# Softmax denominators of 83 of 128 attention units: from four one-column matmuls to a DMA transpose and a VectorE sum

## The chip, the cores and the metric

The kernel runs on one core of a Trainium2 chip. The metric is the device time of one execution in microseconds (us); the median of three runs of the kernel before is 1280.31 us (1280.17 to 1280.67). A profiled execution gives the durations that are used below.

The engines are named as in the profile: PE is TensorE (matmuls), PEld its weight loads, DVE is VectorE, ACT is ScalarE, POOL is GpSimd, and SP is the engine that issues most of the DMAs (SPq is its queue, which works strictly in the order of the program). Each engine works through its own instructions in program order and waits at an instruction until what it needs is there.

## The reference, cut to what matters

```python
xn = layernorm(x)                                   # x: 2048 x 512
q  = (xn @ wq) -> 32 heads x 2048 x 128
p  = softmax(q @ k_cache^T * 128**-0.5)             # 32 heads, 2048 keys
s  = (p @ v_cache) -> 2048 x 4096, then @ wo        # attention
g  = silu(B(xn))                                    # a token-shift mixer and an MLP, gelu
out = x + s * g
```

The change concerns the softmax only. The kernel computes exp(score) without a maximum, multiplies it with V unnormalised, and divides the result afterwards by the sum of the exponentials over the 2048 keys. That sum, the denominator, is one number per query.

## The kernel before, in words

**Units and slots.** The attention is cut into 128 *units* of one head and 512 queries, in the order `units = (g, qt, hh)`: eight groups g of four heads, in each four query blocks qt, in each four heads hh. A unit has eight *slots* (SPU), and a slot treats two key chunks of 128 keys. The main loop (line 695) runs over all 1024 slots n = 8u + p. I write 33.4 for slot 4 of unit 33. What is called from the loop is pinned in program order, so the loop body writes the order of every engine's queue by hand; `at(n, fn)` hangs further work on the end of slot n.

In each slot PE does two score matmuls (`s_slot`, into one of two PSUM tiles of the pool psS; ACT then writes exp of both, 128x1024, into pT) and two matmuls with V (`pv_slot`) of the slot LAG = 5 places earlier, into a PSUM tile `ps_o` (psO, two of them). A pT tile holds two slots; there are four. Further matmuls stand in given slots:

- slots 0 and 1: the query projection of unit u+2 (`q_mm`, four matmuls). `q_copy` brings it to SBUF at slot 2, on DVE, and on ACT for the last units (u+2 > QUIET+1 = 122).
- slot 3: `sums` of unit u-1, four matmuls (below).
- slots 4 and 5: the output projection of an earlier query block (`wo_mm`, four matmuls), evicted by `wo_post` on DVE at slot 6. Such work is put into `wo_todo` after `norm` of a block's fourth head.
- slots 2, 3 and slots 6, 7 are two windows; in each there may be one chunk of the other branch (mixer and MLP), four or five matmuls. There are 136 chunks and some 230 windows. A pair of chunks of the stage m3 (ps_m<-xn2T) ends in a gelu made by hand: `pre` and `square` on ACT, `poly` on DVE two slots later, `tanh` on ACT two slots after that, `last` on DVE after two more. ACT's `tanh` waits for `poly`, and the exponentials stand behind it.

**The denominators.** DVE adds the eight pT quarters of a unit up: `add_first` at slot 4, `add_next` at slot 6, `add_last` (three additions, lines 205, 210, 211) at slot 0 of the next unit. What remains, acc, is 128 keys x 512 queries. `sums` (line 223) multiplies each quarter of acc (128 columns in steps of 4) with a column of ones: four matmuls with one column each, the result 128 x 4 in PSUM. `recip` (line 231) takes the reciprocal on DVE and sends it to DRAM (dr<-rc); `bcast` (line 248, slot 4) reads it back to all 128 partitions (rb<-dr, 128x512); `norm` (line 253) at slot 2 of the unit after multiplies ps_o with rb on DVE and thus frees that PSUM tile for the unit after next.

**PSUM tags.** Two single tiles are left, "xa" and "xm". q_mm, sums and wo_mm share xa; the chunks use xm. From unit 120 on, `sums` uses xm.

**Loads.** K comes by transposing DMAs in four pieces, V in two halves, all issued by SP; a `todo` hung on a slot gives their place in SP's queue. At the start the normalised tokens are turned by SP's transposing DMA too (`ln1_turn`, xnT<-xn); unit 2's slots 6 and 7 hold the first `q_mm` that needs tokens 512 to 1023.

Of the kernel before, what the change touches and what calls it, by code (L numbers as in the profile page):

```python
# [9 lines left out]
ALU = mybir.AluOpType  # L10
FP32 = mybir.dt.float32
# [6 lines left out]
def kernel(  # L18
# [15 lines left out]
    nc = tc.nc  # L34
# [17 lines left out]
    NG = H // HG  # L52

    SPU = KC // 2
    LAG = 5
    KSPLIT = 4
    KJ = KC // KSPLIT
    BASE_J = [3, 3, 2, 2]
# [30 lines left out]
    wqp = ent(pool("wqp", HG + 2))  # L89
    wop = ent(pool("wop", 2 * HG))  # L90
    qtp = ent(pool("qt", 4))
    ptp = ent(pool("pt", 4))
    trp = ent(pool("tr", 2))
    rp = ent(pool("rp", 2))
    otp = ent(pool("ot", 2))
    smp = ent(pool("smp", 4))
    gtp = ent(pool("gt", 2))
# [26 lines left out]
    LQ = QT - 1  # L124
    deferred = {(NG - 2, qt): qt for qt in (LQ - 1, LQ)}
    NS = NU * SPU
    kTs, vBs, wqs, wos, oTs, st = {}, {}, {}, {}, {}, {}
    todo = defaultdict(list)

    def at(n, fn):  # L130
        todo[n].append(fn)
# [35 lines left out]
    def q_mm(u, dcs):  # L167
        g, qt, hh = units[u]
        if dcs[0] == 0:
            st[u] = dict(psq=psX.tile([P, 512], FP32, tag="xm" if u == HG else "xa", name="ps_q"))  # L170
        for dc in dcs:
            mm(st[u]["psq"][:], wqs[g * HG + hh][:, dc, :],
               xnT[:, dc, qt * 512:(qt + 1) * 512], dc == 0, dc == DC - 1)
# [49 lines left out]
    def sums(u):  # L223
# [4 lines left out]
            mm(ps[:, j:j + 1], a[:, j, :], ones_t[:], True, True)  # L228
        recip(s, ps)

    def recip(s, ps):
        rc = smp.tile([P, 4], FP32, name="rc")
        pin(nc.vector.reciprocal(out=rc[:], in_=ps[:]))  # L233
        s["dr"] = drp.tile([P, 4], FP32, name="dr")
        pin(nc.sync.dma_start(out=s["dr"][:], in_=rc[:]))
# [17 lines left out]
    def norm(u, pieces=1):  # L253
        g, qt, hh = units[u]
        s = st.pop(u)
        if hh == 0:
            oTs[(g, qt)] = otp.tile([P, HG, 512], BF16, name="oT")
        w = 512 // pieces
        for i in range(pieces):
            c = slice(i * w, (i + 1) * w)  # L260
            pin(nc.vector.tensor_tensor(  # L261
                out=oTs[(g, qt)][:, hh, c], in0=s["o"][:, c], in1=s["rb"][:, c], op=ALU.mult))
# [94 lines left out]

    def ln1_norm(t):
        xin = ln.pop(t)
        xn = tokp.tile([P, D], BF16, tag="tb", bufs=8, name="xn")  # L360
        norm1(t, xn[:], xin[:])
        return xn

# [121 lines left out]
            lambda: hT[:, 2 * jp:2 * jp + 2, b + tt * 512: b + (tt + 1) * 512])  # L485

    def xn_load(t):
        mlp["xnext"] = tokp.tile([P, D], BF16, tag="tb", bufs=8, name="xr")
        nc.gpsimd.dma_start(out=mlp["xnext"][:], in_=xsrc[t])

    def m2_chunk(t):
# [90 lines left out]
    def m4_chunk(t, part):  # L582
        fcs = list(M4[part])
        ts = t % 4

        def run(i, n):
            if part == 0 and i == 0:
                mlp["ps"] = psX.tile([P, 512], FP32, tag="xm", name="ps_m")
                mlp["xr"] = tokp.tile([P, D], BF16, tag="tb", bufs=8, name="xr")
                nc.gpsimd.dma_start(out=mlp["xr"][:], in_=x1_d[t][:])  # L590
            h = (len(fcs) + 1) // 2
            for fc in (fcs[:h], fcs[h:])[i]:
                mm(mlp["ps"][:], mlp["h2"][fc // 2][:, fc % 2, ts * P:(ts + 1) * P],
                   mlp["w4"][fc][:], fc == 0, fc == FC - 1)
            if part == 2 and i == 1:
                ps, xr = mlp["ps"], mlp["xr"]
                th = tokp.tile([P, D], BF16, tag="th", bufs=1, name="th")

                def x2():
                    pin(nc.vector.scalar_tensor_tensor(  # L600
                        out=xr[:], in0=ps[:], scalar=0.5, in1=xr[:], op0=ALU.mult, op1=ALU.add))

                def tanh():
                    pin(nc.scalar.activation(out=th[:], in_=xr[:], func=ACT.Tanh, scale=0.5))

                def silu():
                    pin(nc.vector.scalar_tensor_tensor(  # L607
                        out=xr[:], in0=th[:], scalar=1.0, in1=xr[:], op0=ALU.add, op1=ALU.mult))
                    nc.gpsimd.dma_start(out=g_d[t][:], in_=xr[:])  # L609

                at(evict(n), x2)
                at(n + 3, tanh)
                at(soft(n + 5), silu)
        return run
# [49 lines left out]
    for t, (stats, apply, turn) in enumerate(tokens, 4):  # L664
# [2 lines left out]
        at(stats, lambda t=t: ln1_stats(t))  # L667
        at(apply, lambda t=t: ln1_apply(t))
        at(turn, lambda t=t: ln1_turn(t))
    for n, h, piece in ((2, 2, 2), (4, 2, 3), (12, 3, 0), (15, 3, 1), (17, 3, 2), (20, 3, 3)):  # L670
        at(n, lambda h=h, piece=piece: load_k(h, (piece,)))
    for n, h, half in ((7, 2, 0), (13, 2, 1), (20, 3, 0), (21, 3, 1)):
        at(n, lambda h=h, half=half: load_v(h, (half,)))
    at(28, ph1_load)
    at(64, w2_load)
# [2 lines left out]
    for g in range(NG - 1):  # L678
        b = (g * QT + QT - 1) * HG
        for hh in range(HG):  # L680
            h = (g + 1) * HG + hh
            for i in range(KSPLIT):
                at((b - 2 + (2 * hh + i // 2 + (hh > 0))) * SPU + (5, 7)[i % 2], lambda h=h, i=i: load_k(h, (i,)))
            for i in range(2):
                at((b - 2 + (2 * hh + i + (hh > 0))) * SPU + 6, lambda h=h, i=i: load_v(h, (i,)))
            at((b + (-4, -4, -1, -1)[hh]) * SPU + (5, 7)[hh % 2], lambda h=h: load_w(h))
            at((b - 4 - hh // 2) * SPU + (5, 7)[hh % 2], lambda h=h: load_wo(h))

# [3 lines left out]
            at((QUIET + 1 + 2 * (t % 4)) * SPU + 4, lambda t=t: gate_sum(t))  # L692

    wo_todo = deque()
    for n in range(NS):
        u, p = divmod(n, SPU)
        s_slot(u, p)
        m = n - LAG
        if m >= 0:
            pv_slot(*divmod(m, SPU))  # L700
        if u == 0 and p in (1, 3, 5):
            q_mm(1 + p // 2, range(DC))
        if u == 0 and p in (2, 4, 6):
# [8 lines left out]
            add_last(u - 1)  # L712
        if p == 2 and HG - 1 <= u < NU - 2:
            q_copy(u + 2)
        if p == 2 and u >= 2:
            norm(u - 2)
            gg, qq, hh = units[u - 2]
            if hh == HG - 1 and (gg, qq) in deferred:
                pin(nc.sync.dma_start(out=o_d[qq][:], in_=oTs[(gg, qq)][:]))
            elif hh == HG - 1:  # L720
                wo_todo.extend((gg, 4 * qq + ts) for ts in range(4))
                if gg == NG - 1:
                    fin_load(4 * qq)
        if p == 3 and u >= 1:
            sums(u - 1)
        if p == 4 and u >= 1:
            bcast(u - 1)
        if p in (4, 5) and wo_todo:
            wo_mm(*wo_todo[0], (0, 1) if p == 4 else (2, 3))
        if p == 6 and QUIET <= u < NU - 1:  # L730
            add_next(u, 2)
        if p == 6 and wo_todo:
            gg, t = wo_todo.popleft()
            wo_post(gg, t)
            if gg == NG - 1:
                at(n + 5, lambda t=t: wo_out(t))
                if t % 4 < 3:
                    fin_load(t + 1)
        if p == 4:
            add_first(u)  # L740
        if p == 4 and u == NU - 1:
            a = st[u]["acc"]
            pin(nc.vector.tensor_tensor(out=a[:, 0:2, :], in0=a[:, 0:2, :], in1=a[:, 2:4, :], op=ALU.add))
        if p == 6 and u < QUIET:
            add_next(u, 2)
        if p in (2, 3, 6, 7):
# [54 lines left out]
        wo_part(dst[j], GL, ts[j], range(HG), False, True)  # L801
    for j in range(4):
        last_scale(ts[j], dst[j])
        if j < 2:
            last_out(ts[j], nc.gpsimd)
    for j in (2, 3):
        last_out(ts[j], nc.vector)
    ph.close()

# [29 lines left out]
```

## Time and profile before

| what | value |
|---|---|
| median of 3 runs | 1280.31 us |
| the profiled execution's own time | 1279.53 us |
| its span in the trace | 1277.8 us |
| granted TensorE clock, mean | 0.999 |
| PSUM sum matmuls (ps_sum<-ones_t,acc) | 516 of them, 171 ns each, 34.3 us busy |
| multiply by the reciprocal (oT<-ps_o,rb, 128x512) | 127 of them, 680 ns each |
| transposing DMAs SBUF to SBUF (xnT<-xn, xn2T<-x1r) | 12 and 16, 3.8 us to landing in the median |
| transposing DMAs of K | 128, 4.7 us to landing in the median |

Matmuls are pipelined: one of 512 columns lasts 0.38 us in the records, but the next begins 0.216 us later. A PE that is called busy is therefore read by its starts: a stretch in which every 512-column matmul starts 0.216 us after the one before has no wait in it. A row of the timeline joins instructions of one kind that follow each other (x2, x4) and shows the time from the first start to the last end.

### The profile page before, as it was taken

What the parts mean: (1) busy time and instruction counts of PE and PEld (TensorE: products, weight loads), DVE (VectorE), ACT (ScalarE), POOL (GpSimd) and SP (SyncE); (2) the same over time, 40 slices, a digit from 0 to 9 for tenths busy, and PEclk for the clock granted to TensorE, in tenths of its full rate; (3) what the DMA queues carried; (4) which work ended last, traced back from release to release, by engine and by line L of the source; (5) the groups of instructions that cost most, each with busy time, mean ns of one, the idle gap of its engine ahead of it and who ended that gap; (6) DMA issues with size and microseconds to landing.
All of it is one profiled execution on the core that took longest, in us unless ns stands there. A gap on an engine that the chain in (4) does not pass through costs nothing.

```text
span 1277.8 us, 17233 instructions
## 1 busy us (share of the span) xinstructions
PE 1257.1 (98%) x6195; PEld 612.1 (48%) x6320; DVE 1019.2 (80%) x1407; ACT 1113.0 (87%) x1195; POOL 137.9 (11%) x241
## 2 busy tenths in 40 slices
PE   8999999999999999999999999999999999999998
PEld 5444444444444444444444444444444444444444
DVE  7888889898788877778887778887777888777886
ACT  7899998888999988899988889998888999888883
POOL 4430003323110010000001000000000000000110
PEclk9999999999999999999999999999999999999999
DMA  9644343455532564134443244523435133542532
GB/s 185 133 106 81 59 79 88 108 124 123 115 77 67 100 110 89 42 75 83 89 93 68 58 85 93 96 42 75 96 80 90 34 70 72 91 105 46 140 76 58
DMA packets 172950, 111.79 MB, mean 87 GB/s; under 512 B 124800, under 2 KB 149888, under 8 KB 172864
## 3 DMA queue, kind: packets, MB, share of 16 engines
q1 hardware_dynamic: 163904, 85.51, 34.3%
q0 software_dynamic: 8672, 24.91, 7.9%
q8 instruction: 49, 0.80, 0.3%
q14 instruction: 37, 0.30, 0.1%
q10 hardware_dynamic: 288, 0.26, 0.1%
HBM read 82.58 MB, written 7.60 MB: 71 GB/s over the span
## 4 chain that ended last, share of the span: by engine, by line
PE 87%; ACT 6%; DVE 4%; issue 1%; DMA 1%; POOL 0%; DVEq 0%; ACTq 0%
PE ps_s L114 31%; PE ps_o L114 30%; PE ps_m L114 9%; PE ps_wo L114 8%; PE ps_q L114 7%; ACT pT L194 4%; PE ps_sum L114 1%; ACT sq L425 1%; DVE acc L205 1%; ACT pre L455 1%; DVE bn L349 0%; DMA rb<-dr 0%; DMA xnT<-xn 0%; DVE acc L210 0%; DVE qT L180 0%
## 5 line engine op out<-in xcount | busy, mean ns | idle before, releaser
L194 ACT ACTIVATE pT<-ps_s 128x1024 bf16<-128x1024 f32 x1024 | 1012.0, 1031 | 141.0 <-PE ps_s L114 130.0
L114 PE MATMUL ps_s<-qT,kT 128*128 128x512 bf16 x2004 | 599.5, 379 | 4.1 <-ACT pT L194 1.0
L114 PE MATMUL ps_o<-pT,vb 128*128 128x512 bf16 x1997 | 597.6, 379 | 2.8
L205 DVE TENSOR_TENSOR acc<-acc,pT 128x2048 bf16<-128x2048 bf16 x254 | 309.8, 1220 | 65.5 <-ACT pT L194 60.8
L114 PEld LDWEIGHTS <-kT 128*128 128x128 bf16 x2048 | 226.8, 113 | 224.4 <-issue 18.6
L114 PEld LDWEIGHTS <-vb 128*128 128x128 bf16 x2048 | 199.8, 98 | 225.2
L200 DVE TENSOR_TENSOR acc<-pT 128x2048 bf16<-128x2048 bf16 x128 | 155.9, 1218 | 26.6 <-ACT pT L194 26.4
L114 PE MATMUL ps_q<-xnT,wq_h 128*128 128x512 bf16 (+1 forms) x519 | 150.7, 374 | 3.3 <-DMA xnT<-xn 2.0
L114 PE MATMUL ps_wo<-wo_h,oT 128*128 128x512 bf16 x456 | 136.3, 379 | 0.6
L328 DVE TENSOR_TENSOR s_acc<-ps_wo,s_acc 128x512 f32<-128x512 f32 x100 | 68.9, 689 | 73.9 <-PE ps_wo L114 71.0
L210 DVE TENSOR_TENSOR acc<-acc 128x1024 bf16<-128x1024 bf16 x127 | 87.9, 692 | 4.4
L261 DVE TENSOR_TENSOR oT<-ps_o,rb 128x512 bf16<-128x512 f32 x129 | 87.1, 676 | 4.1 <-DMA rb<-dr 4.0
L180 DVE CAST qT<-ps_q 128x512 bf16<-128x512 f32 x122 | 83.5, 685 | 4.8 <-PE ps_q L114 4.8
L114 PEld LDWEIGHTS <-wq_h 128*128 128x128 bf16 x524 | 50.6, 98 | 63.2 <-issue 3.6
L114 PEld LDWEIGHTS <-oT 128*128 128x128 bf16 x480 | 46.9, 98 | 57.7 <-issue 2.6
L114 PE MATMUL ps_m<-xn2T,w_sb 128*128 128x512 bf16 x222 | 66.1, 378 | 0.2
L114 PE MATMUL ps_m<-w_sb,h2T 128*128 128x512 bf16 x218 | 62.7, 379 | 0.2
L577 POOL DMA_DIRECT2D w_sb<-in_B_w_dram x28 | 21.1, 756 | 353.8 <-PE ps_m L114 328.6
L211 DVE TENSOR_TENSOR acc<-acc 128x512 bf16<-128x512 bf16 x127 | 54.0, 425 | 4.3
L233 DVE RECIPROCAL rc<-ps_sum 128x4 f32<-128x4 f32 x128 | 22.9, 179 | 40.9 <-PE ps_sum L114 40.0
L114 PEld LDWEIGHTS <-acc 128*128 128x128 bf16 x516 | 37.6, 115 | 29.6 <-issue 1.5
L609 POOL DMA_DIRECT2D g_d<-xr x16 | 8.8, 547 | 346.3 <-DVE xr L607 346.3
(74 smaller groups left out, 599.9 us busy)
## 6 DMA issues: line engine op xcount, KB each, us to landing
rb<-dr SPq DMA_DIRECT2D x128, 256.0 KB, 4.1
vb<-in_A_v_cache_dram SPq DMA_DIRECT2D x64, 256.0 KB, 4.5
w_sb<-in_B_w_dram POOLq DMA_DIRECT2D x28, 256.0 KB, 4.6
wo_h<-in_A_wo_dram SPq DMA_DIRECT2D x32, 128.0 KB, 3.9
wq_h<-in_A_wq_dram SPq DMA_DIRECT2D x28, 128.0 KB, 4.2
kT<-in_A_k_cache_dram SPq DMA_TRANSPOSE x128, 4.7
dr<-rc SPq DMA_DIRECT2D x128, 2.0 KB, 1.4
xr<-in_A_x_dram POOLq DMA_DIRECT2D x16, 128.0 KB, 3.5
```

What stands on the lines that cost most here:

```text
L114: pin(nc.tensor.matmul(out=out, lhsT=lhsT, rhs=rhs, start=start, stop=stop))
L180: pin(nc.vector.tensor_copy(out=qT[:], in_=st[u].pop("psq")[:]))
L194: pin(nc.scalar.activation(out=s["pT"][-1][:, jj:jj + 2, :], in_=sps[:], func=ACT.Exp, scale=SCALE))
L200: pin(nc.vector.tensor_tensor(out=s["acc"][:], in0=s["pT"][0][:], in1=s["pT"][1][:], op=ALU.add))
L205: pin(nc.vector.tensor_tensor(out=a[:], in0=a[:], in1=st[u]["pT"][i][:], op=ALU.add))
L210: pin(nc.vector.tensor_tensor(out=a[:, 0:2, :], in0=a[:, 0:2, :], in1=a[:, 2:4, :], op=ALU.add))
L211: pin(nc.vector.tensor_tensor(out=a[:, 0, :], in0=a[:, 0, :], in1=a[:, 1, :], op=ALU.add))
L233: pin(nc.vector.reciprocal(out=rc[:], in_=ps[:]))
L261: pin(nc.vector.tensor_tensor(out=oTs[(g, qt)][:, hh, c], in0=s["o"][:, c], in1=s["rb"][:, c], op=ALU.mult))
L328: pin(nc.vector.tensor_tensor(out=sa, in0=ps[:], in1=sa, op=ALU.add))
L425: pin(nc.scalar.activation(out=sq[:], in_=pre[:], func=ACT.Square, scale=GELU_A ** 0.5))
L577: pin(nc.gpsimd.dma_start(out=w[:], in_=w3_v[:, :, fc * P:(fc + 2) * P]))
```

## The change

Units T0 = 32 to T1 - 1 = 114, 83 of them, are "turned". For these, `sums` is not called. Instead the folded acc (128 keys x 512 queries, bf16) is transposed by a DMA that SP issues at slot 2 of the next unit (`acc_turn`); at slot 6 DVE adds each of the 4 x 128 rows up along the keys (`turned_sums`), then `recip` as before. `bcast` moves from slot 4 of the next unit to slot 1 of the unit after, `norm` from slot 2 to slot 6 of that unit. Query q = 128 j + p now lies at place 4 p + j of rb, so that `norm` reads rb in steps of four.

Because `norm` comes later, V matmuls run up to eight slots behind: the lag grows 5, 6, 7, 8 in slots 33.1, 33.3 and 33.5, and shrinks again in 117.3, 117.7 and 118.3. pT has five tiles instead of four; rb one instead of two; the token tiles "tb" four instead of eight. V halves of three of a group's four heads are hung three slots later. `wo_post` asks whether a projection is in PSUM (wo_box) rather than whether one is to be done. The last query projections (u > 122) use tag xm instead of xa. Three of the first loads move to later slots, and of the last four output additions one instead of two is on POOL.

```diff
-    LAG = 5
-    ptp = ent(pool("pt", 4))
+    ptp = ent(pool("pt", 5))
-    rp = ent(pool("rp", 2))
+    rp = ent(pool("rp", 1))
+    atp = ent(pool("at", 1))
+    T0, T1 = 8 * HG, NU - 13
+    LAGS = [((T0 + 1) * SPU + 1, 5), ((T0 + 1) * SPU + 3, 6), ((T0 + 1) * SPU + 5, 7),
+            ((T1 + 2) * SPU + 3, 8), ((T1 + 2) * SPU + 7, 7), ((T1 + 3) * SPU + 3, 6), (NS, 5)]
...
-            st[u] = dict(psq=psX.tile([P, 512], FP32, tag="xm" if u == HG else "xa", name="ps_q"))
+            st[u] = dict(psq=psX.tile([P, 512], FP32, tag="xm" if u == HG or u > QUIET + 1 else "xa", name="ps_q"))
...
+    def turned(u):
+        return T0 <= u < T1
+
+    def acc_turn(u):
+        s = st[u]
+        s["at"] = atp.tile([P, 4, P], BF16, name="accT")
+        pin(nc.sync.dma_start_transpose(out=s["at"][:], in_=s["acc"][:, 0, :]))
+
+    def turned_sums(u):
+        s = st[u]
+        sm = smp.tile([P, 4], FP32, name="sm")
+        pin(nc.vector.tensor_reduce(
+            out=sm[:], in_=s.pop("at")[:], axis=mybir.AxisListType.X, op=ALU.add))
+        recip(s, sm)
...
+        if turned(u):
+            f = "x (j p) -> x j p"
+            pin(nc.vector.tensor_tensor(
+                out=oTs[(g, qt)][:, hh, :].rearrange(f, j=4), in0=s["o"].rearrange(f, j=4),
+                in1=s["rb"].rearrange("x (p j) -> x j p", j=4), op=ALU.mult))
+            return
...
-    for n, h, piece in ((2, 2, 2), (4, 2, 3), (12, 3, 0), (15, 3, 1), (17, 3, 2), (20, 3, 3)):
+    for n, h, piece in ((2, 2, 2), (4, 2, 3), (14, 3, 0), (16, 3, 1), (17, 3, 2), (20, 3, 3)):
-    for n, h, half in ((7, 2, 0), (13, 2, 1), (20, 3, 0), (21, 3, 1)):
+    for n, h, half in ((7, 2, 0), (15, 2, 1), (20, 3, 0), (21, 3, 1)):
...
-                at((b - 2 + (2 * hh + i + (hh > 0))) * SPU + 6, lambda h=h, i=i: load_v(h, (i,)))
+                at((b - 2 + (2 * hh + i + (hh > 0))) * SPU + (9 if hh else 6), lambda h=h, i=i: load_v(h, (i,)))
...
-        m = n - LAG
-        if m >= 0:
-            pv_slot(*divmod(m, SPU))
+        lag = next(v for lim, v in LAGS if n < lim)
+        while pv_done <= n - lag:
+            pv_slot(*divmod(pv_done, SPU))
+            pv_done += 1
...
-        if p == 2 and u >= 2:
+        if u >= 1 and p == 2 and turned(u - 1):
+            acc_turn(u - 1)
+        if u >= 2 and p == 1 and turned(u - 2):
+            bcast(u - 2)
+        if u >= 2 and p == (6 if turned(u - 2) else 2):
             norm(u - 2)
...
-        if p == 3 and u >= 1:
+        if p == 3 and u >= 1 and not turned(u - 1):
             sums(u - 1)
-        if p == 4 and u >= 1:
+        if p == 4 and u >= 1 and not turned(u - 1):
             bcast(u - 1)
...
-        if p == 6 and wo_todo:
+        if p == 6 and wo_box:
             gg, t = wo_todo.popleft()
             wo_post(gg, t)
...
+        if p == 6 and u >= 1 and turned(u - 1):
+            turned_sums(u - 1)
         if p == 6 and u < QUIET:
             add_next(u, 2)
...
     for j in range(4):
         last_scale(ts[j], dst[j])
-        if j < 2:
+        if j == 0:
             last_out(ts[j], nc.gpsimd)
-    for j in (2, 3):
+    for j in range(1, 4):
         last_out(ts[j], nc.vector)
```

More of the change, by code (lines that the diff above doesn't have):

```diff
@@ L359, in ln1_norm @@
         xin = ln.pop(t)
-        xn = tokp.tile([P, D], BF16, tag="tb", bufs=8, name="xn")
+        xn = tokp.tile([P, D], BF16, tag="tb", bufs=4, name="xn")
         norm1(t, xn[:], xin[:])
@@ L487, in xn_load @@
     def xn_load(t):
-        mlp["xnext"] = tokp.tile([P, D], BF16, tag="tb", bufs=8, name="xr")
+        mlp["xnext"] = tokp.tile([P, D], BF16, tag="tb", bufs=4, name="xr")
         nc.gpsimd.dma_start(out=mlp["xnext"][:], in_=xsrc[t])
@@ L588, in run @@
                 mlp["ps"] = psX.tile([P, 512], FP32, tag="xm", name="ps_m")
-                mlp["xr"] = tokp.tile([P, D], BF16, tag="tb", bufs=8, name="xr")
+                mlp["xr"] = tokp.tile([P, D], BF16, tag="tb", bufs=4, name="xr")
                 nc.gpsimd.dma_start(out=mlp["xr"][:], in_=x1_d[t][:])
@@ L694 @@
     wo_todo = deque()
+    pv_done = 0
     for n in range(NS):
```

## The prediction

> **What bounds the kernel now.** I read the page's busy shares and its chain of work, then the timeline unit by unit.
>
> ```profile
> PE 1257.1 (98%) x6195; PEld 612.1 (48%) x6320; DVE 1019.2 (80%) x1407; ACT 1113.0 (87%) x1195; POOL 137.9 (11%) x241
> ...
> PE 87%; ACT 6%; DVE 4%; issue 1%; DMA 1%; POOL 0%; DVEq 0%; ACTq 0%
> ```
>
> The chain runs through PE. Counting PE's weight loads unit by unit gives the test: number of 512-column matmuls times 0.216 us, plus the four sum matmuls, against the unit's length. Most units agree within 0.02 us (unit 23: 44 x 0.216 + 0.13 = 9.63 of 9.63); others exceed it by 0.1 to 0.3. So a matmul taken away shortens the run, except where PE already waits. What a denominator costs is seen in unit 34, slots 2 to 4:
>
> ```profile
> 342.63 1.94 ACT L194 ACTIVATE pT<-ps_s 128x1024 bf16<-128x1024 f32 x2 [0.33 <-PE ps_s L114]
> 342.80 0.59 PE L114 MATMUL ps_s<-qT,kT 128*128 128x512 bf16 x2
> ...
> 343.23 0.59 PE L114 MATMUL ps_o<-pT,vb 128*128 128x512 bf16 x2
> 343.45 0.40 PEld L114 LDWEIGHTS <-acc 128*128 128x128 bf16 x4
> 343.66 0.27 PE L114 MATMUL ps_sum<-ones_t,acc 128*128 128x1 bf16 x4
> 343.76 0.15 PEld L114 LDWEIGHTS <-kT 128*128 128x128 bf16 x2
> 343.79 0.60 PE L114 MATMUL ps_s<-qT,kT 128*128 128x512 bf16 x2
> ```
>
> The scores follow the first sum by 343.79 - 343.66 = 0.13 us: four one-column matmuls at 0.033 each, not the 171 ns of the table. That, not 34 us, is at stake.
>
> **A. The sums removed.** 83 x 0.13 = 10.9 at most. But a score pair may not start before the exponential two slots earlier has ended, plus 0.05 us (the least distance in the trace). Above, that exponential ends at 342.63 + 1.03 = 343.66, so without the sums the scores start at 343.71 instead of 343.66: a gain of 0.08. In 49 of the slots after a removed sum the distance is 0.75 or more (a chunk filled slots 2, 3): 49 x 0.131 = 6.4; in 34 it is short and 0.07 to 0.09 is left: 2.7. Together **-9.1**.
>
> **B. The lag.** In 33.1, 33.3 and 33.5 no V pair is issued; 3 x 0.432 = 1.30 us of PE work is done later, in 117.3 to 118.3. Unit 33 cannot use the free time: ACT runs without a pause from 33.1 to 33.6 (ACT is busy 9.80 of the unit's 9.84 us). Following its exponentials, PE leaves unit 33 only 0.27 earlier, of which 0.07 stands in A. **+1.1** (0 to 1.3).
>
> **C. The first loads.**
>
> ```profile
> 29.54 1.19 SPq L370 DMA_TRANSPOSE xnT<-xn  x1
> ...
> 33.98 0.59 PE L114 MATMUL ps_q<-xnT,wq_h 128*128 128x512 bf16 x2 [1.96 <-DMA xnT<-xn]
> ...
> 35.55 1.12 SPq L146 DMA_TRANSPOSE kT<-in_A_k_cache_dram  x1
> 36.73 1.08 SPq L156 DMA_DIRECT2D vb<-in_A_v_cache_dram  x2
> ```
>
> PE waits 2 us for the last token block. Taking a K piece (1.25 of SP) and a V half (0.6 and the gap) out of SP's way brings its turn 2.0 earlier, from 29.54 to 27.5. What is late next: V of head 3 is issued at 36.73 and lands 4.5 later, 41.2, behind the same sum of SP work as now; PE's first V matmul of unit 3 stands at 41.80. So only some 0.5 survives; **-0.4** (0 to -2.0).
>
> **D. Output projections** come one unit later for turned blocks. Mostly a swap; unit 109, which waits 0.59 for ACT with only four matmuls in slots 4 and 5, gets four more there. **-0.5** (0 to -0.6).
>
> **E. The end of attention.** q in tag xm no longer waits for the eviction of xa (0.46 of excess in each of 123.0 and 125.0): -0.9. But the sums of these units are in xm too, and stand after q:
>
> ```profile
> 1200.40 0.59 PE L114 MATMUL ps_o<-pT,vb 128*128 128x512 bf16 x2
> 1200.71 0.59 ACT L178 ACTIVATE qT<-ps_q 128x512 bf16<-128x512 f32 x1
> 1200.83 0.27 PE L114 MATMUL ps_sum<-ones_t,acc 128*128 128x1 bf16 x4
> ...
> 1215.40 0.59 PE L114 MATMUL ps_q<-xnT,wq_h 128*128 128x512 bf16 x2 [0.51 <-DVE s_acc L328]
> ```
>
> The sums must now await q's copy: 1200.71 + 0.59 + 0.05 - 1200.83 = 0.5 in units 121 to 125, everything on PE behind them: +2.6. Net **+1.7**. The last additions: POOL's cost 1.15, DVE's 0.68 without POOL beside it (692 ns for an fp32 addition); three in a row on DVE end about 0.15 later: **+0.15** (-0.4 to +0.4).
>
> **F. What DVE and SP get.** Per turned unit DVE loses nothing (the reciprocal stays) and gets a sum over 128x512 bf16. The trace has no such operation; rows with 512 elements take 425 (bf16 addition) to 689 ns (eviction), a statistics pass over 512 bf16 679. I take 0.68, being a reduction too; upper end 1.22, the row of twice the elements. The multiply reads rb in steps of 16 bytes: no VectorE row has steps. The nearest is a PE weight load, 113 ns in steps (kT) against 98 (vb), so 0.68 x 1.15 = 0.78; ends 0.68 and, twice as long, 1.36. It moves into the 0.75 to 1.3 us in which DVE idles before the eviction of slot 6, so it costs little even then. DVE's average load rises from 40.4 to about 44 of 49 us in the five heaviest units, 33 to 37. But order matters:
>
> ```profile
> 366.91 0.69 DVE L328 TENSOR_TENSOR s_acc<-ps_wo,s_acc 128x512 f32<-128x512 f32 x1 [1.30 <-PE ps_wo L114]
> ...
> 367.72 1.22 DVE L205 TENSOR_TENSOR acc<-acc,pT 128x2048 bf16<-128x2048 bf16 x1
> ...
> 368.86 1.22 DVE L429 SCALAR_TENSOR_TENSOR sq<-sq,pre 128x1024 bf16<-128x1024 bf16 x1
> ...
> 370.27 1.10 ACT L434 ACTIVATE sq<-sq 128x1024 bf16<-128x1024 bf16 x1
> ```
>
> Sum and reciprocal (0.71 + 0.10) come between the first two rows, which have 0.2 of slack: poly ends 0.6 later, at 370.68. Tanh, now 0.2 behind poly, starts 0.47 later, the exponentials behind it too, and PE waits 0.28 for the second (372.29 + 0.47 + 0.05 against 372.53). Eight m3 pairs close in slots 2, 3 with this slack of 0.20; the other four have 0.5 to 0.8 and the 16 in slots 6, 7 at least 1.0 with norm gone from before poly. 8 x 0.28 = **+2.2** (0 to +4).
>
> SP's queue gets 83 transposes of 1.2 us issue each; a unit has 9.6 and no unit fills it. Their path: add_last ends (362.56 in unit 36), landing 3.8 later in the median of the SBUF transposes (2.4 to 6.2), DVE wants the data at 367.5, 4.9 after. rb is issued some 2 us after the reciprocal, lands 4.1 later and is wanted 7 after. Each psO tile is free more than a slot before V needs it at lag 8. So all of it is hidden: 0, with the next paragraph's rival behind it. DMA shares are 0.42 and rise by 83 x 0.66 / 1278 = 4 points (512 packets of about 20 ns on 16 engines).
>
> **Sum**: -9.1 + 1.1 - 0.4 - 0.5 + 1.7 + 0.15 + 2.2 = -4.85. The profiled execution took 1279.53 (span 1277.8), so 1274.7; the median of runs lies 0.8 above it, so **1275.4**.
>
> **Rivals.** *Late transposes (slower).* The turn waits for DVE, lands, and DVE waits for it with everything behind it: add_next, poly, so ACT's tanh and the exponentials. Up to 4.9 us of landing is free (4.3 after a gelu). From then on each us hits the 12 pairs of slots 2, 3; at 5.4 the gain is gone (12 x 0.4), at 5.8 as a median 0.9 is late: 12 x 0.8 = 9.6, 1285; beyond 6 the 16 other pairs join. For: K's median is 4.7, its longest 7.0. Against: SBUF sources 3.8. Chance 0.16.
>
> *DVE dearer than rows of 512 elements.* With 1.22 for the sum, poly is 0.54 later still: 8 x 0.54 + 4 x 0.4 = 5.9, so 1281; with 1.36 for the multiply alone, 1 at most, in units like 33. Chance 0.15 between 1277.5 and 1282. [...]
>
> *ACT as the bound.* If in the 47 turned units with m3 chunks (ACT 94% busy) nothing were gained, A shrinks by about 5: 1280.3. Against: PE's starts follow at 0.216 in most of their slots. Chance 0.08.
>
> *Better.* If poly's delay hides and the start gains 2.0: 1275.4 - 2.2 - 1.6 = 1271.6. Chance 0.14 below 1273.
>
> Forecast itself, 1273 to 1277.5: 0.47. A run of this kernel can tell 0.2%, 2.6 us. Faster by more (below 1277.75): 0.47 + 0.14 + 0.02; slower (above 1282.9): the late transposes, 0.15; the rest, 0.22, within. The range takes in the better case and the dear sum: 1271 to 1282.5.
>
> **What would show it.** Right: no ps_sum between 33.3 and 115.3; units without a gelu 0.13 or 0.08 shorter; a wait of ps_sum in 121 to 125; tanh of eight pairs starting 0.5 later; accT landing near 3.8. Wrong: DVE's sum waiting for accT, a multiply over 1 us, score pairs waiting for ACT in most units.

## The result, and the profile after

The changed kernel takes 1285.91 us in the median (1283.88 to 1287.36, six runs), the kernel before 1280.49 (1279.83 to 1281.34) beside it: a ratio of 1.0042 (1.0032 to 1.0052). It is slower by 5.4 us, where 4.9 less was forecast. The profiled execution took 1285.89, its span is 1284.1 and its mean granted clock 0.997.

The page's busy shares and chain of work, in answer to the two lines of before:

```profile
PE 1253.0 (98%) x5870; PEld 602.0 (47%) x5988; DVE 1096.0 (85%) x1491; ACT 1113.4 (87%) x1195; POOL 137.7 (11%) x240
...
PE 70%; ACT 10%; DVE 8%; DMA 7%; issue 3%; SPq 1%; POOL 0%; DVEq 0%; ACTq 0%
```

PE's sums are gone from the matmul count, but the share of PE in the chain fell from 87% to 70%; ACT, DVE and DMA took it. DVE has 77 us more to do. So PE does less and waits more. Where, the length of stretches of units tells (from the weight loads of the unit's first score matmuls, as in the prediction). The same table serves the experiments:

| kernel (profiled execution) | 0-5 | 6-32 | 33-115 | 116 | 117-118 | 121-125 |
|---|---|---|---|---|---|---|
| before | 52.67 | 266.36 | 819.75 | 8.99 | 19.46 | 45.67 |
| **after** | 57.28 | 266.38 | 816.10 | 11.60 | 20.76 | 47.02 |
| after_again | 53.47 | 266.41 | 822.64 | 10.63 | 20.76 | 47.03 |
| after_third | 53.49 | 266.36 | 819.67 | 10.78 | 20.76 | 47.03 |
| before_nosums | 52.95 | 266.40 | 810.74 | 8.99 | 19.46 | 45.67 |
| before_lags | 53.02 | 266.40 | 820.31 | 9.02 | 20.75 | 45.64 |
| after_freered | 53.38 | 266.40 | 815.45 | 9.06 | 20.76 | 47.03 |
| after_bare | 52.76 | 266.36 | 811.92 | 9.02 | 20.76 | 45.65 |
| after_late_units | 53.06 | 266.34 | 815.96 | 9.02 | 19.50 | 45.65 |

After against before: +4.61 at the start, -3.65 in the units with removed sums, +2.61 in unit 116, +1.30 where the lag shrinks, +1.35 at the end; together +6.2 of the 6.36 between the two profiled executions. Three places of it need their lines.

**The turned units.** The sums are gone as meant. Unit 34 again, slots 1 to 3, from the timeline: the scores follow each other at once.

```profile
346.50 0.38 PE L114 MATMUL ps_s<-qT,kT 128*128 128x512 bf16 x1
...
347.36 0.59 PE L114 MATMUL ps_s<-qT,kT 128*128 128x512 bf16 x2
```

The distance from 346.50 to 347.36 is four matmuls of 0.216 (two of scores, two with V) and nothing else. But two units on, DVE is late. The timeline of units 34 to 37, DVE, SP, ACT and PE in order of time (start, duration, instruction, idle time before it and what ended it); the write of unit 33's reciprocals (dr) and its broadcast (rb) come first:

```profile
353.11 0.32 SPq L253 DMA_DIRECT2D dr<-rc  x1
353.47 1.13 SPq L149 DMA_TRANSPOSE kT<-in_A_k_cache_dram  x1
357.31 0.32 SPq L268 DMA_DIRECT2D rb<-dr  x1
...
361.96 1.08 DVE L278 TENSOR_TENSOR oT<-ps_o,rb 128x512 bf16<-128x512 f32 x1 [1.76 <-DMA rb<-dr]
...
368.78 0.42 DVE L214 TENSOR_TENSOR acc<-acc 128x512 bf16<-128x512 bf16 x1
369.24 1.21 SPq L240 DMA_TRANSPOSE accT<-acc  x1
...
373.75 0.69 DVE L245 TENSOR_REDUCE sm<-accT 128x4 f32<-128x512 bf16 x1 [1.23 <-DMA accT<-acc]
...
375.68 1.22 DVE L453 SCALAR_TENSOR_TENSOR sq<-sq,pre 128x1024 bf16<-128x1024 bf16 x1
...
377.00 1.06 ACT L458 ACTIVATE sq<-sq 128x1024 bf16<-128x1024 bf16 x1 [1.92 <-DVE sq L453]
377.96 2.84 ACT L197 ACTIVATE pT<-ps_s 128x1024 bf16<-128x1024 f32 x3
...
379.02 0.59 PE L114 MATMUL ps_s<-qT,kT 128*128 128x512 bf16 x2 [1.66 <-ACT pT L197]
```

The same places in the kernel before, unit 33's write and broadcast and the end of unit 35's additions:

```profile
344.18 0.32 SPq L235 DMA_DIRECT2D dr<-rc  x1
345.58 0.32 SPq L250 DMA_DIRECT2D rb<-dr  x1
345.95 1.12 SPq L146 DMA_TRANSPOSE kT<-in_A_k_cache_dram  x1
...
362.14 0.42 DVE L211 TENSOR_TENSOR acc<-acc 128x512 bf16<-128x512 bf16 x1
```

This is a cascade. It begins at rb: in the changed kernel a K piece now stands between write and broadcast, the write of units 32 and 33 lands after 3.95 and 4.14 us (1.40 and 1.39 before), and rb, which waits for it, is issued 4.2 after the write instead of 1.4. In the two other profiles of the changed kernel below these landings are 3.1 to 4.5. That the K piece slows the write is not shown; and late writes alone do not stop PE, since after_bare (below) has them too, 4.23 and 3.80, and exceeds its matmuls by only 0.26 and 0.43 in units 36 and 37. The multiply of unit 33 then waits 1.76 for rb; everything that DVE has behind it is late, the additions of unit 35 too. They end 6.3 us into unit 36, where in the kernel before they ended 4.0 into it. So the transpose is issued late (369.24), lands 4.5 later (the median of all 83 is 3.6), and the sum waits 1.23 for it. Poly stands behind the sum, ACT's tanh waits 1.92 for poly, the exponentials stand behind tanh, and PE waits 1.66.

**Unit 116.** A late accT meets the change back to matmul sums:

```profile
1146.20 1.23 SPq L240 DMA_TRANSPOSE accT<-acc  x1
...
1152.21 0.69 DVE L245 TENSOR_REDUCE sm<-accT 128x4 f32<-128x512 bf16 x1 [1.98 <-DMA accT<-acc]
...
1156.65 0.68 DVE L183 CAST qT<-ps_q 128x512 bf16<-128x512 f32 x1
1157.39 0.27 PE L114 MATMUL ps_sum<-ones_t,acc 128*128 128x1 bf16 x4 [2.42 <-DVE qT L183]
```

The last transpose lands 6.0 after its issue, the sum waits 1.98, the copy of q comes late, and the first matmul sums after the turned units share tag xa with that q: 2.42 of waiting.

**The start.** The timelines of SP and of PE:

```profile
36.87 0.32 SPq L268 DMA_DIRECT2D rb<-dr  x1
...
38.42 1.08 SPq L159 DMA_DIRECT2D vb<-in_A_v_cache_dram  x2
```

```profile
39.94 0.59 PE L114 MATMUL ps_s<-qT,kT 128*128 128x512 bf16 x2
44.04 1.03 PE L114 MATMUL ps_o<-pT,vb 128*128 128x512 bf16 x2 [3.51 <-DMA vb<-in_A_v_cache_dram]
44.87 1.06 PE L114 MATMUL ps_s<-qT,kT 128*128 128x512 bf16 x2
```

V of head 3 was issued at 38.42 (36.73 before) and landed 5.6 later instead of 4.5; PE, which no longer waits 2 us for the tokens, was there at 40.5 and idled for 3.51. After that two matmuls take 0.83 from start to start instead of 0.43. The busy time of the engines in stretches of 2 us says why (after the five engines: granted clock, share of the DMA engines, GB/s):

```profile
44.00:46.00 2.00, 1.96 (x5) 0.73 (x6) 1.97 (x5) 0.03 (x1) 0.41 (x1) 0.50 0.36 64
46.00:48.00 2.00, 2.00 (x6) 0.75 (x5) 0.60 (x1) 1.32 (x2) 1.85 (x3) 0.50 0.35 49
```

The granted clock fell to 0.50 at 43.3, while PE still idled, and stayed there for 6.83 us. PE was at work in 6 of them, at half its rate, which costs another 3.0 (an estimate: half of 6).

The measured prices of the new operations, from the page's groups (count, then busy time and mean ns, then idle time before them):

```profile
L278 DVE TENSOR_TENSOR oT<-ps_o,rb 128x512 bf16<-128x512 f32 x83 | 89.2, 1075 | 17.5 <-DMA rb<-dr 17.5
L245 DVE TENSOR_REDUCE sm<-accT 128x4 f32<-128x512 bf16 x83 | 56.3, 678 | 4.1 <-DMA accT<-acc 3.9
```

The sum takes 678 ns, the multiply with rb in steps of 16 bytes 1075 instead of 680; and DVE waits 17.5 us for rb (23 times), where the multiplies of the kernel before waited 3.6 in all.

### The profile page after: what moved, and what is told of

The parts are those of the page before. It is cut to its first block, busy times and chain, and to the rows that moved or that the text cites. A ratio compares the mean times of both kernels' runs of the same rounds, so it can differ in the third digit from the quotient of the medians.

```text
span 1284.1 us, 16634 instructions
## 1 busy us (share of the span) xinstructions
PE 1253.0 (98%) x5870; PEld 602.0 (47%) x5988; DVE 1096.0 (85%) x1491; ACT 1113.4 (87%) x1195; POOL 137.7 (11%) x240
## 4 chain that ended last, share of the span: by engine, by line
PE 70%; ACT 10%; DVE 8%; DMA 7%; issue 3%; SPq 1%; POOL 0%; DVEq 0%; ACTq 0%
PE ps_s L114 26%; PE ps_o L114 25%; ACT pT L197 8%; PE ps_m L114 7%; PE ps_wo L114 7%; PE ps_q L114 6%; DVE acc L208 3%; DMA accT<-acc 2%; DMA dr<-rc 2%; DMA rb<-dr 2%; ACT pre L479 1%; DVE sm L245 1%; ACT sq L458 1%; DVE acc L213 1%; DVE oT L278 1%
## 5 line engine op out<-in xcount | busy, mean ns | idle before, releaser
L114 PEld LDWEIGHTS <-kT 128*128 128x128 bf16 x2048 | 229.8, 113 | 240.0 <-issue 29.9
L278 DVE TENSOR_TENSOR oT<-ps_o,rb 128x512 bf16<-128x512 f32 x83 | 89.2, 1075 | 17.5 <-DMA rb<-dr 17.5
L245 DVE TENSOR_REDUCE sm<-accT 128x4 f32<-128x512 bf16 x83 | 56.3, 678 | 4.1 <-DMA accT<-acc 3.9
L453 DVE SCALAR_TENSOR_TENSOR sq<-sq,pre 128x1024 bf16<-128x1024 bf16 x36 | 43.8, 1216 | 0.0
```

The costliest lines, as they stand in the source:

```text
L114: pin(nc.tensor.matmul(out=out, lhsT=lhsT, rhs=rhs, start=start, stop=stop))
L245: pin(nc.vector.tensor_reduce(out=sm[:], in_=s.pop("at")[:], axis=mybir.AxisListType.X, op=ALU.add))
L278: pin(nc.vector.tensor_tensor(out=oTs[(g, qt)][:, hh, :].rearrange(f, j=4), in0=s["o"].rearrange(f, j=4), in1=s["rb"].rearrange("x (p j) - ...
L453: pin(nc.vector.scalar_tensor_tensor(out=sq[:].rearrange(f2), in0=sq[:].rearrange(f2), scalar=1.0, in1=pre[:].rearrange(f2), op0=ALU.add, ...
```

## The experiments

Three theories followed from these lines. *Late VectorE*: the sums were worth what was forecast, and the gain is lost in the turned units because VectorE waits for transfers, with poly, q_copy and the last sums behind it. *The loads* (rival): the moved first loads cost most of it. *No gain* (rival): the sums were never worth 9, since the score pairs wait for ACT. The kernel before, run beside every series of the experiments, had medians of 1280.05 to 1280.21, so the ratio to it is given only where it decides something.

### Terms A and C alone, in the kernel before

before_nosums leaves out the sums of units 32 to 114 (their denominators are a constant):

```diff
-            sums(u - 1)
+            if 32 <= u - 1 < 115:
+                recip(st[u - 1], None)      # reciprocal of a constant tile
+            else:
+                sums(u - 1)
```

> The kernel before, with the four sum matmuls of units 32 to 114 left out and their reciprocal taken of a constant on VectorE (so these denominators are not computed); nothing else is changed. Theory: the forecast's term A is right, and the loss comes from what was put in the place of the sums. Then 9.1 us are gained here: 1271.4, at most 10.9. Rival: the sums stood in waits that come back elsewhere, term A was too large; then 0 to 4 us are gained, 1276.5 to 1280.5.

before_newloads takes over only the moved first loads:

```diff
-    for n, h, piece in (... (12, 3, 0), (15, 3, 1), ...):
+    for n, h, piece in (... (14, 3, 0), (16, 3, 1), ...):
-    for n, h, half in (... (13, 2, 1), ...):
+    for n, h, half in (... (15, 2, 1), ...):
```

> The kernel before, with only the three first loads in their new slots. Theory: the first wait for the tokens becomes shorter by some 1.6 us, but the first V half of head 3 arrives late for it, TensorE waits about 3.5 us and then runs at half its clock for some 5 us; the run is 4 to 5 us longer: 1285. Rival: the start of the profiled run was disturbed by chance or by another part of the change (fewer token tiles, one tile for the broadcast); then the moved loads alone change the time by -2 to +0.5: 1278.5 to 1281.

Measured: without the sums 1271.16 (1270.2 to 1272.16), ratio 0.9929 (0.9917 to 0.9940): -8.9, and -9.01 in units 33 to 115 of the profile. Term A (-9.1) holds and *no gain* falls. The moved loads: 1279.58, ratio 0.9999 (0.9990 to 1.0007), eleven of twelve runs between 1278.8 and 1280.3 and one at 1284.5. In the kernel before, *the loads* are thus no cost of every run; what they cost in the changed kernel is another question.

### Two parts of the change undone: old first loads, and a contiguous multiply

> The changed kernel with the three first loads back in their old slots. Theory: the 4.8 us that the changed kernel is behind at the start of unit 6 go away: 1281.1, and no wait of a V matmul for its DMA in unit 3. Rival: the start is as late as in the changed kernel, 1285.9, because another part of the change makes it so.

after_plainmult reads rb contiguously, so that a query is divided by another query's denominator:

```diff
-                in1=s["rb"].rearrange("x (p j) -> x j p", j=4), op=ALU.mult))
+                in1=s["rb"].rearrange(f, j=4), op=ALU.mult))
```

> The changed kernel, in which the multiply of the turned units reads the broadcast reciprocals one after the other instead of in steps of 16 bytes (so each query is divided by another query's denominator). Theory: the multiply takes 0.68 us again instead of 1.075, VectorE is 83 x 0.4 = 33 us less busy, and of the stalls in units 36, 37, 61, 64, 85 and 108, together 5 us, half or more go, and part of the 2.6 us of unit 116: 1281 to 1283. Rival: the stalls come from the order of VectorE's queue and from late transposes and not from the multiply's length: within 1 us of the changed kernel, 1285 to 1286.5.

Measured, on one chip: old loads 1280.59 (1277.2 to 1283.4), as its theory said, and contiguous read 1276.77 (1275.5 to 1282.0), 4 below its theory. Both are below the changed kernel, the second although it keeps the moved loads. With the contiguous read the multiply is back at 685 ns and DVE's waits for rb fall from 17.5 us to 5.0. So by the medians the 33 us of DVE time that the steps cost (83 x 0.395) are not hidden. The two profiles do not show it: units 33 to 115 take 813.7 with the contiguous read and 814.3 with the old loads, whose profiled execution (1277.2) is the fastest of its twelve.

### What accT's latency costs, the lag alone, and q back in xa

after_again is the changed kernel as the line of comparison on this chip; before_lags is the kernel before with the lags, five pT tiles and four token tiles of the changed kernel; after_qxa is the second cut below; after_freered lets VectorE add up the folded sum itself (other denominators):

```diff
-        out=sm[:], in_=s.pop("at")[:], axis=mybir.AxisListType.X, op=ALU.add))
+        out=sm[:], in_=s["acc"][:, 0, :].rearrange("k (j p) -> k j p", j=4), axis=..., op=ALU.add))
```

> The changed kernel once more, as the line of comparison for the other three on the same chip. Its first six runs lay between 1283.9 and 1287.4 with a mean granted clock of 0.997 to 0.998, while the same kernel with the old slots of the first loads had 1277.2 to 1283.4 and, in its faster runs, 0.999 to 1.000. Theory (the start of the changed kernel has two outcomes: V of head 3 lands either in time, or so late that PE idles some 4 us and then gets half its clock for some 5 us): the runs fall into two heaps about 4 to 5 us apart, the lower near 1281 with a clock of 0.999, the upper near 1286 with 0.997. Rival (the moved loads cost this in every run of the changed kernel, though not in the kernel before): all runs at 1284 to 1287 and 0.997 again.

> The transposes are still issued, but VectorE adds up the folded sum itself, 128x512 bf16 that is there already, and does not wait for accT; the denominators are thus other sums than the reference's, the amount of work is the same. Theory (part of the missing gain lies in sums that wait for a late accT, with q_copy, poly and so tanh and the last non-turned sums behind them): stalls in units 37, 108 and 116 go, 3 to 5 us faster than the changed kernel on the same chip and start. Rival (accT is not what is late; VectorE is late by its own load and the dear multiply): less than 1 us, and the same stalls.

> The kernel before with only the lag grown to eight from unit 33 on and shrunk again in 117 and 118, five tiles of pT and four token tiles. Theory (term B): the three V pairs that were left out in unit 33 are done in 117 and 118, +1.1 (0 to 1.3). Rival (the longer lag lets PE run free of the exponentials, or holds PSUM longer: norm at slot 2 comes just when V of the unit before ends at lag 8): a loss of 0.3 and more in many units, or a gain below 0.

```diff
-    psX.tile([P, 512], FP32, tag="xm" if u == HG or u > QUIET + 1 else "xa", name="ps_q")
+    psX.tile([P, 512], FP32, tag="xm" if u == HG else "xa", name="ps_q")
```

> The changed kernel with the last query projections back in tag xa. Theory (term E as the profile after shows it: 121 to 125 last 9.23 each, where two of them had 8.78 and the others 9.24 before): 1.35 faster than the changed kernel, the sums of 121 to 125 start without waiting for the copy of q. Rival: the eviction of xa comes later in the changed kernel and q waits for it by more than 0.46, so nothing or a loss.

Measured: changed kernel 1286.21 (1283.4 to 1290.6), without the wait for accT 1279.41 (1277.1 to 1284.8), the lag alone 1281.87 (ratio to before 1.0014, 1.0006 to 1.0023), q in xa 1287.56 (1281.3 to 1291.4).

- accT: 6.8 less, more than the theory's 3 to 5. Unit 116 is back at 9.06, so its 1.6 to 2.6 belong to the late accT. *Late VectorE* is supported. Not every stall goes: units 36 and 37 still exceed their matmuls by 0.56 and 0.87, and DVE still waits 18.2 us for rb in the turned units.
- The lag: +1.7, of which the profile shows 1.29 in 117 and 118 and 0.56 in 33 to 115. Forecast were +1.1, at most 1.3.
- q: the medians tell nothing, with runs that lie 10 us apart. The profile does: 121 to 125 take 45.64 instead of 47.03, -1.39. The wait that goes is the forecast one, here in unit 123 of the changed kernel:

```profile
1224.20 0.59 ACT L181 ACTIVATE qT<-ps_q 128x512 bf16<-128x512 f32 x1
1224.85 0.27 PE L114 MATMUL ps_sum<-ones_t,acc 128*128 128x1 bf16 x4 [0.30 <-ACT qT L181]
```

The profile of after_again tells more than its time. Its start went well (53.47, V of head 3 waited 2.2, no fall of the clock), and yet it took 1287.53: units 33 to 115 cost 822.64, more than before the change. Between three profiles of the same kernel this stretch takes 816.1, 819.7 and 822.6. The expectation that the runs fall into two heaps by the start alone is therefore wrong; the turned units scatter as much.

### The sum behind poly, a write in the order of the queries, and the costs undone together

after_redlast moves sum and reciprocal one slot on (their place in the loop body is then behind `acc_turn`); after_scatter writes the reciprocals to DRAM in the order of the queries, so that the multiply reads rb contiguously; after_bare undoes all four costs; after_best joins old loads, q in xa and the write in order.

```diff
-        if p == 6 and u >= 1 and turned(u - 1):
+        if p == 7 and u >= 1 and turned(u - 1):
             turned_sums(u - 1)
```

> The changed kernel with VectorE's sum and reciprocal one slot later, at slot 7, so that they stand behind poly in VectorE's order instead of ahead of it. Theory (a late accT costs time because poly, and so ACT's tanh and the exponentials, stand behind the waiting sum): the stalls at slot 3 of units such as 37, 42, 59, 64, 108 (0.5 to 3 us each in the profiles of the changed kernel, some 3 us in one, 9 in the other) go, 3 us or more faster than the changed kernel's 6 above the kernel before. Rival (the lateness only moves on): the reciprocal comes 1.2 to 2.5 later, rb is issued some 2 us after it and lands 4.3 later, so the multiply at slot 6 waits for rb in most units, about 1.5 us each, and its tile ps_o and VectorE's queue behind it make PE wait: as slow as the changed kernel or slower, by up to 83 x 0.3 = 25.

```diff
-        pin(nc.sync.dma_start(out=s["dr"][:], in_=rc[:]))
+        dst = s["dr"][:].rearrange("p j -> (p j)").rearrange("(j p) -> p j", j=4)
+        pin(nc.sync.dma_start(out=dst, in_=rc[:]))          # turned units only
```

> The changed kernel with the reciprocals written to DRAM in the order of the queries (512 pieces of 4 bytes instead of 128 of 16), so that the multiply reads rb contiguously; nothing of the computation changes. Theory (the dear multiply, 1075 against 680 ns, takes 33 us of VectorE in 83 units and with it the slack that a late accT or rb would need): the multiply is back at 0.68, and about 3 us are gained against the changed kernel, as with the contiguous read of the wrong order. Rival (the small pieces make the way of the reciprocal through DRAM longer by 1 us and more, and the multiply waits for rb instead): no gain or a loss.

> The changed kernel without the four costs found so far: the first loads at their old slots, the last q in xa, a contiguous read of rb (each query is divided by another query's denominator) and VectorE's sum over the folded sum itself, without waiting for accT (other sums than the reference's); the transposes are still issued. Theory (the terms add up): 1280.2 - 8.9 (sums) + 1.7 (lag) - 0.5 (unit 109) = 1272.5, at most 1274, and runs within 3 us of each other. Rival (the gain of the sums is lost to something else in the turned units, the transposes' traffic or ACT): 1276 or more.

> The changed kernel with the first loads at their old slots, the last q in xa and the reciprocals written in the order of the queries with a contiguous read of rb; it computes what the reference does. Theory: 1280.2 - 8.9 + 1.7 - 0.5 and 1 to 3 for late accT = 1273.5 to 1275.5, faster than both kernels. Rival (the small pieces delay rb): 1277 or more.

**after_redlast**: 1332.98. The rival decides: rb is late instead. The waits of its profile (in all, times, longest):

```profile
DVE oT L278 <- DMA rb<-dr: 130.2, 77, 4.0
...
ACT sq L458 <- DVE sq L453: 24.9, 13, 3.9
...
PE ps_o L114 <- DVE oT L278: 20.2, 22, 2.1
```

The multiply waits for rb in 77 of 83 units, and tanh waits longer than ever, since poly stands behind the multiply too. One slot (1.2 us) of delay in this loop makes the run 53 us longer than the kernel before and 44 to 47 longer than the changed kernel's medians, where the rival had at most 25; so there was next to no slack in the way from the sum to rb.

**after_scatter** 1898.81 and **after_best** 1896.43, some 620 us more than the kernel before: a write in 512 pieces of 4 bytes took 9.4 us to land in the median of the 83 (8.9 in that of all 128 writes of after_scatter), one in 128 pieces of 16 bytes 1.4 in the changed kernel. SP's queue shows it; rb can be issued 10.1 after the write instead of the 1.4 to 4.8 of the changed kernel:

```profile
377.51 0.36 SPq L256 DMA_DIRECT2D dr<-rc  x1
387.59 0.33 SPq L271 DMA_DIRECT2D rb<-dr  x1
```

Both rivals named the direction and neither the size.

**after_bare**: 1273.93 (1273.1 to 1276.1), ratio 0.9955 (0.9943 to 0.9968), within the 1272.5 to 1274 of the theory, and its runs lie 3 us apart. The terms add up to within 1.4 us. Units 33 to 115 take 811.92, so the changed kernel loses 4.2, 10.7 and 7.8 us in them in its three profiles. The other kernels with the same turned units lose 2.3 (after_oldloads), 7.6 (after_qxa) and 12.3 (after_two_undone, below). Unit by unit the place is the same in all six: units 67 to 107 together last as long as in after_bare to 0.02 us, and the loss lies in 33 to 66 (1.8 to 9.9) and 108 to 115 (0.5 to 2.6).

### A correct contiguous read, and the undone parts together

after_permadd has the last addition of 128x512 bf16 read both operands in steps of four elements, so that the sums come out in the order of the queries; the transpose then takes `acc[:, 2, :]`, and the multiply reads rb contiguously. after_two_undone has the old loads and q in xa, after_best3 both of these and the addition in steps.

```diff
+        if turned(u):
+            t = "k (p j) -> k j p"
+            pin(nc.vector.tensor_tensor(
+                out=a[:, 2, :].rearrange("k (j p) -> k j p", j=4), in0=a[:, 0, :].rearrange(t, j=4),
+                in1=a[:, 1, :].rearrange(t, j=4), op=ALU.add))
+            return
```

> The changed kernel a third time, as the line of comparison for the next three on the same chip: 1283 to 1288 as on two chips before, with a mean granted clock of 0.997 to 0.998 in the runs whose start goes wrong.

> The changed kernel, but VectorE's last addition (128x512 bf16) reads its two operands in steps of four elements of 2 bytes, so that the sums come out in the order of the queries and the multiply reads rb contiguously; the result is the reference's, the multiply is 0.68 again. Theory (the steps of 16 bytes of the multiply cost; steps of 8 bytes in an addition of bf16 cost at most what an addition of fp32 takes, 0.69 instead of 0.42): VectorE gets 0.395 - 0.27 = 0.13 per unit back, the multiply ends earlier but accT starts 0.27 later, so nothing to 2 us faster than the changed kernel. Rival (the two inputs in steps are dearer than one: 1.1 and more): accT lands 0.7 later, VectorE gains nothing, slower than the changed kernel by 2 to 5.

> The changed kernel with the first loads at their old slots and the last q in xa. Theory (the two terms add up): 1.35 from q, and 4 to 5 from the start in those runs of the changed kernel whose clock falls; so 1279 to 1280.5, level with the kernel before, and mean clocks of 0.999 to 1.000 in most runs. Rival (the start is left to chance by the kernel's other edits, four token tiles for instance): the same scatter of clocks as the changed kernel, and 1.35 alone is gained.

> All three together: old first loads, last q in xa, and the last addition in steps so that the multiply is contiguous; it computes what the reference does. Theory: the kernel before less 8.9 (sums) less 0.5 (unit 109) plus 1.7 (lag) plus 2 to 4 for late accT and rb: 1274.5 to 1276.5, faster than both kernels. Rival (the addition in steps is as dear as the multiply was): 1278 to 1280.

Measured, on one chip: changed kernel 1288.85 (1283.0 to 1289.7), contiguous multiply 1283.07 (1280.6 to 1285.8), old loads and q in xa 1282.79 (1279.7 to 1289.9; its theory had 1279 to 1280.5, its rival a gain of 1.35 alone, and it met neither), all three 1280.57 (1278.5 to 1284.9), ratio to before 1.0001. The group of that addition:

```profile
L216 DVE TENSOR_TENSOR acc<-acc 128x512 bf16<-128x512 bf16 x83 | 57.5, 692 | 2.8
```

The multiply is back at 685. The addition costs 692 instead of 425, as the theory took it, and the transpose starts that much later. The gain of 5.8 is above the theory's 0 to 2 even so; five runs of a kernel that scatters by 7 us do not give it exactly. The combination misses its 1274.5 to 1276.5 and comes out just above its rival's 1278 to 1280: with the undone parts the mean clocks are mostly 0.999 to 1.000, and still units 33 to 115 take 822 in its profile. (The profiled execution, 1284.87, is the longest of its eleven.) The latency stays, and with it the cascade. In after_two_undone the granted clock fell to 0.50 too, in a stall of 3.15 us in unit 37 (clock third from the end):

```profile
374.00:376.00 2.00, 0.00 (x0) 0.00 (x0) 2.00 (x2) 0.93 (x1) 0.00 (x0) 1.00 0.05 4
...
378.00:380.00 2.00, 2.00 (x6) 0.64 (x5) 1.83 (x2) 1.18 (x2) 0.00 (x0) 0.50 0.33 66
```

### Turning only the units that can bear it

```diff
-    T0, T1 = 8 * HG, NU - 13
+    T0, T1 = 17 * HG, NU - 22
```

> The changed kernel with only units 68 to 105 turned (38 of 83; the 45 others add up with matmuls as before), old first loads, last q in xa; it computes what the reference does, with the multiply in steps of 16 bytes. Theory (the gain of a removed sum is real, about 0.107 each, and is lost only where poly, q_copy's matmul behind it or the change back to matmul sums stands behind a late accT, which in all profiles is in units 33 to 66 and 108 to 116): 1280.15 - 38 x 0.107 + 1.7 (lag) = 1277.8, and runs within 3 us of each other like those of the kernel before. Rival (the waits go where the turned units are): stalls of 1 to 2 in 68 to 72 and 105 to 110, 1280 or more, and a scatter of 6 us.

It also has the old first loads and the last q in xa, so it is to be compared with after_two_undone, from which it differs in T0 and T1 alone.

Measured: 1276.62 (1276.01 to 1277.04), ratio 0.9972 (0.9961 to 0.9983): faster than both kernels, with all seven runs within about 1 us. after_two_undone, with 83 turned units, was 2.6 above the kernel before beside it. The dear multiply, the latency of accT (3.4 in the median, though never above 4.8, where the changed kernel had up to 6.0) and the same order on DVE are all still there. PE's waits are short:

```profile
PE ps_q L114 <- DMA xnT<-xn: 1.8, 1, 1.8
...
PE ps_s L114 <- ACT pT L197: 1.2, 5, 0.3
PE ps_sum L114 <- DVE qT L183: 1.1, 2, 0.9
```

What is left are the waits of the start, as before, and small ones; ACT's tanh waits 0.5 for poly in all (4.9 in the changed kernel), and DVE waits for rb 5.2 us in its 38 multiplies instead of 17.5 in 83. So the stalls belong to the place, the units 33 to 66 and 108 to 116, and not to the turned units as such. It came out 1.2 better than its theory. Two places account for it: unit 69, where three V pairs are left out, takes 8.46 instead of 9.84, because ACT has room there (7.66 of the 8.46), where in unit 33 the same omission gave PE 0.27; and unit 109 no longer exceeds its matmuls, which it did by 0.59 before.

## Why the prediction was wrong, point by point

- **A** was right: -9.1 forecast, -8.9 and -9.0 measured alone.
- **B** was right in mechanism and too small: +1.1 (0 to 1.3) forecast, +1.7 measured alone. Its reason, that unit 33 cannot use the free time, is confirmed by unit 69, which can.
- **C** failed in its tail. "Only some 0.5 survives" is what the loads alone give in the kernel before (-0.5, not told from 0). What the step left out is that PE then waits for V instead of for the tokens. In the profiled execution V landed a microsecond later (5.6 after its issue instead of 4.5), the wait lasted 3.51 us, and within it the granted clock fell to 0.50: +4.6. It does not happen in every run: the two other profiles of the changed kernel, where this wait is 2.2, start without a fall of the clock. The mean clock of 0.997 to 0.998 in all of its first six runs, against 0.999 to 1.000 in the profiles that show no such fall, fits one in each, but only one of them has a profile. The runs with the contiguous multiply, which keep the moved loads, look like it too: eight with 0.999 to 1.000 at 1275.5 to 1277.6, four with 0.997 to 0.998 at 1279.6 to 1282.0. How much of the median the loads carry is not settled: in the last comparison, undoing them and q (1.4) gave 6.1 against the changed kernel and 2.5 in the pair with a contiguous multiply, so 1 to 5.
- **D** was right in unit 109, whose excess over its matmuls fell from 0.59 to 0.04. Part of it came back in unit 108, which exceeds its matmuls by 1.38, by 1.08 to 1.23 in the other two profiles and, without the late accT and the dear multiply, still by 0.70.
- **E** was right: +1.7 forecast, +1.35 to 1.39 measured, and by the forecast wait.
- **F** is the step that failed. Its prices were good: the sum 0.678 for 0.68; the multiply 1.075, dearer than the 0.78 taken, but inside the ends 0.68 and 1.36 (the upper one the author's estimate); the trace has it at 1.58 times the 680 ns of the contiguous read before. What failed are three sentences. "It moves into the 0.75 to 1.3 us in which DVE idles before the eviction of slot 6, so it costs little even then": it does not, since the contiguous read gained 3.8 against the old loads' kernel on one chip and 5.8 on another against the changed kernel. And "so all of it is hidden: 0": each transfer was compared with its own due time, 4.9 for accT against 3.8, and about 7 for rb against 6.1, with DVE taken to be on time. The third is "rb is issued some 2 us after the reciprocal": in units 32 and 33 it was over 4, because the write between them landed after 3.95 and 4.14. The two transfers and DVE form a loop. The multiply waits for rb, the additions behind it come late, the next transpose is issued late, the sum waits for it, rb is late again. Slacks of 1 us in each arm are one common slack, which the late write, the dear multiply and the added sum use up in units 33 to 37, where DVE is busy 43.6 of 50.5 us. That the slack is common is read from the order of the timeline; that each arm counts is measured: a shorter multiply, no wait for accT, and one slot of delay each moved the time.
- The forecast loss of 2.2 (eight pairs at 0.28) became 4.2 to 10.7 in units 33 to 115 and 1.6 to 2.6 in unit 116. The rival of late transposes named this path, DVE's sum with poly and tanh behind it, and set its price on a median landing of 5.8. The median was 3.6: in units 35 to 37 it was the issue that came late, and only single landings were long (5.5 for unit 34, 6.0 for unit 114). The handover in unit 116 was not seen at all: what shares tag xa with a matmul sum was checked for the tail and not for the last turned unit.
- With the stalls taken as measured, the profiled execution of the result adds up: -6.2 (after_bare: sums, lag and D), +1.4 for q, +4.6 at the start, +4.2 in units 33 to 115 and +2.6 in unit 116 give +6.6, against the +6.36 measured. What stays open is why the cascade is so different between executions of one kernel (816.1, 819.7, 822.6). That DMA landings differ a little from run to run and a loop with no slack enlarges it is argued, not shown.

## What to carry to other kernels

When work is moved from a busy engine into a round trip (engine, DMA, engine, DMA, engine), add up the slack of the whole loop and not of each transfer, and look at what stands behind each wait in the waiting engine's order. Use the slack where it is: with the first loads and the last q as before, 38 turned units in the light part of the kernel gained 3.5 us, and 83 with the heavy part lost 2.6. A change that makes the runs scatter has put the kernel on the edge of a wait; then compare unit by unit in profiles, since medians of a few runs no longer tell 1 us.

## What the runs showed of the hardware that was not expected

- **The granted clock of PE fell to one half within idle times of 3.15 and 3.51 us.** In the changed kernel the half rate began 2.7 us into an idle time of 3.51 us and lasted 6.83; in after_two_undone it began 2.6 us into one of 3.15 and lasted 3.4. Not every idle time did this: 2.42 us in unit 116 of the changed kernel and 1.96 at the start of the kernel before left the clock at 1.00. What decides it is not shown. The stall of 3.15 us cost some 1.4 more than its own length (an estimate: half of the 2.9 us in which PE then worked at half rate).
- A multiply of 128x512 with one fp32 operand in steps of 16 bytes took 1075 ns in the changed kernel instead of 680 before; an addition of 128x512 bf16 with both operands in steps of 8 bytes took 692 in after_permadd instead of 425.
- Writing 2 KB from SBUF to DRAM in 512 pieces of 4 bytes landed after 9.4 us in the median of the 83 in after_scatter (8.9 in the median of all its 128 writes); in 128 pieces of 16 bytes after 1.4 in the changed kernel, but after 3.95 and 4.14 in its units 32 and 33 (3.1 to 4.5 over its three profiles).
